# In 11 of 64 attention units, one maximum step that takes two key blocks

## The chip, the cores and the metric

The kernel runs on one core of a Trainium2 chip. A core has five engines with a queue of instructions each: TensorE (PE, matrix products into PSUM), VectorE (DVE), ScalarE (ACT), GpSimd (POOL, no access to PSUM here) and SyncE (SP, which issues DMA transfers). They run at the same time and wait for one another through semaphores. The metric is the time of one execution on the device in microseconds (us); lower is better.

## The reference

The kernel computes one transformer block on x of 2048 tokens by 512 channels, in bfloat16: layer norm, attention with 32 heads of 16 channels, a projection with a residual, layer norm, and a gated feed-forward part of 1792 channels with a residual. Cut to what matters:

```python
q, k, v = qkv[0], qkv[1], qkv[2]
scores = jnp.einsum("bhqd,bhkd->bhqk", q, k) * (Dh ** -0.5)
p = _softmax(scores, axis=-1)
o = jnp.einsum("bhqk,bhkd->bhqd", p, v)
...
h = x + _A_ref(_layernorm(x, axis=-1), A_wqkv, A_wo)
h2 = h + _B_ref(_layernorm(h, axis=-1), B_w_gate, B_w_up, B_w_down)
```

where `_B_ref` is `(gelu(x @ w_gate) * (x @ w_up)) @ w_down`. The softmax needs, for each query and head, the maximum of 2048 scores.

## The kernel before, in words

**Units.** Attention is cut into 64 units. A unit is 256 queries (one of 8 groups `gi`) by 4 heads (one of 8 `slot`s; the heads' 16 channels sit in row groups of 32 partitions). Each unit goes through two passes.

**Pass 1, the maxima.** For each of 16 steps j, two matmuls (`p1_pair`, L797) write the scores of 128 queries and 512 keys for two heads into two PSUM banks, and VectorE takes both maxima in one reduction of 128 x 1024 (`p1_consume`, L806). The step's number says which block it is: key block kc = j // 4 (of four), query tile qh = (j // 2) % 2, head pair j % 2. GpSimd joins the four key blocks' maxima (`negm_part`, `negm_pre`), writes the negative maximum as three bfloat16 parts, has it transposed by a DMA (`negm_post`, L846) and adds it to spare rows of the queries (L851), so that a later product of keys and queries gives the score less the maximum.

**Pass 2, the exponentials.** 24 ticks after a unit's first maximum step, its scores are computed again with keys as rows (`p2_tile`, L867), and ScalarE takes the exponential of 128 x 512 per tile (`p2_consume`, L879). The tiles go into a ring of 34 buffers; `item_pv` (L893) multiplies them with the values (a column of ones gives the sums). Every other unit, `item_ofin` turns the result with fp32 transposes on TensorE (L919), ScalarE copies it (OAT, L641), and GpSimd divides by the sums with a power of -1 (L928) and a product (L932).

**Ticks.** The main loop from L1293 writes out one tick per maximum step: first the scores of pass 1, then two tiles of pass 2, then one piece of a dense stream (`Dense.piece`): projections of queries, keys and values, the value products, the output projection, and the gate, up and down products of the feed-forward part of an earlier group. If no piece may start, `dummy` (L1285) puts in matmuls without a use. PSUM has eight banks: two pairs for pass 1 in turn, four for pass 2 and the dense pieces together. The order of each engine's instructions is fixed when the program is built. A planner decides it with estimated costs: `act_lag` counts how far ScalarE would be behind at 1.135 us a tick, and gate and up pieces start only under `LAG_START`; `PoolStream` has a budget for GpSimd; `defer` places an operation some ticks later; `ADDX` is the delay before L851.

**The end.** After the last maximum step, 24 ticks of exponentials are left, then `tail_a` and `tail_b`: the last normalisation, output projection, layer norm and feed-forward part of the last group, with `fill` putting pieces or dummies into TensorE's waits. `FILL_2` and `FILL_LN` say how many. `evac_act` (L641) copies out of PSUM on ScalarE, or on VectorE (L630) once the maxima are done.

Of the kernel before, what the change touches and what calls it, by code (L numbers as in the profile page):

```python
# [222 lines left out]
ADDX = 4  # L223
# [3 lines left out]
FILL_2 = 4  # L227
FILL_LN = 16
LAG_START = 0.4
LAG_OP = 0.2  # L230
TANH_LAG = 2


def bass_sequential_preLN__mha_block__geglu_ffn__prompt_kernel(nc, A_x, A_wqkv, A_wo, B_x, B_w_gate, B_w_up, B_w_down, out):
    dbg = None
    with ExitStack() as es:
# [74 lines left out]
        OAT = at("OAT", [128, 2, 272], FP32)  # L311
# [189 lines left out]
        def startable(it, room):  # L501
            if it[0] is item_gate and par_busy[it[1][1] % 2] and room < 10:
                return False
            if it[0] is item_down and it[1][0] == GL - 1 and not force[0]:
                return False
# [4 lines left out]
        class Dense:  # L510
            def __init__(self):
                self.prio = []
                self.ready = []
                self.gen = None
                self.bank = None
                self.banks = [7, 3, 4, 5]
                self.rr = 0
                self.pause = 0
                self.single = False
                self.done = 0  # L520
                self.now = 0
# [6 lines left out]
            def _start(self, item):  # L528
                genfn, a, est, nb = item
                if self.single:  # L530
# [5 lines left out]
            def piece(self):  # L536
                if self.single and self.pause > 0:
                    return 0
                while True:
                    if self.gen is None:  # L540
# [4 lines left out]
                        if self.prio and (not self.single or self.prio[0][3] <= self.now):  # L545
                            self._start(self.prio.pop(0))
                        elif self.ready and (not self.single or ((act_lag[0] <= LAG_START or force[0] or self.ready[0][0] not in (item_gate, item_up)) and startable(self.ready[0], lim - self.now) and self.ready[0][3] <= self.now and self.now + self.ready[0][2] + PAUSE - 1 <= lim)):
# [3 lines left out]
                    try:  # L551
# [11 lines left out]
                        if self.single:  # L563
                            banks.give(self.bank)
                            self.pause = PAUSE
# [7 lines left out]
        dense = Dense()  # L573

# [19 lines left out]
        class PoolStream:  # L594

            def __init__(self):
                self.q = []
                self.budget = 0.0
            def add(self, ops, then=None):
# [4 lines left out]
            def spend(self, cost):  # L604
                self.budget -= cost
            def run(self, flush=False):
                while self.q and (flush or self.budget >= min(self.q[0][0], 1.0)):
                    if not flush and self.q[0][0] > 2.0 and dense.now % 16 in (1, 2, 3, 13, 14, 15):
                        break
                    cost, fn, then = self.q.pop(0)  # L610
                    self.budget -= cost
                    fn()
# [190 lines left out]
        def p1_consume(ui, tiles):  # L803
            par = ui % 2
            (b, qt, kc, g), (b2, _, _, g2) = tiles
            P.op("dve", lambda e: e.tensor_reduce(out=PM[:, par, qt, kc, g:g + 2], in_=pbank[:, b:b + 2, :], axis=AX.X, op=ALU.max),  # L806
                 reads=[("pb", b), ("pb", b2)], writes=[("PM", par, qt, kc, g), ("PM", par, qt, kc, g2)])

        def negm_part(ui, k):
# [10 lines left out]
            else:  # L820
# [3 lines left out]
                P.op("pool", lambda e: e.tensor_scalar(out=m3, in0=m3, scalar1=-1.0, scalar2=None, op0=ALU.mult), reads=[("MXm", par)], writes=[("MXm", par)])  # L824

# [16 lines left out]
        def negm_post(ui):  # L842
# [10 lines left out]
            defer(ADDX, add)  # L853
# [6 lines left out]
        def p2_tile(ui, j, gp, jj):  # L860
# [3 lines left out]
            m, g, b = j // 2, 2 * gp + jj, banks.take()  # L864
# [5 lines left out]
            return (b, m, g)  # L870

# [10 lines left out]
        def item_pv(b, ui):  # L882
# [18 lines left out]
            evac_act(OA[:, par, 256 * col:256 * col + 256], pbank[:, b, 0:256], [("pb", b)], [("OA", par, col)], cost=0.41)  # L901
            if gi == GL and slot >= NSLOT - 2:
                if col == 0:
                    dense.add(item_ofin, gi, (slot,), front=True, est=3, not_before=dense.now + 3)
            elif col == 1:
                dense.add(item_ofin, gi, (slot - 1, slot), front=True, est=3, not_before=dense.now + 3)
# [6 lines left out]
        oat_busy = {}  # L913
        def item_ofin(b, gi, slots):
            gp, par, ns = gi % 2, slots[0] // 2 % 2, len(slots)
            assert not oat_busy.get(par), "GpSimd too far behind"
            for q in range(2):
                for sp in range(ns):
                    P.op("pe", lambda e, q=q, sp=sp: e.transpose(out=pbank[:, b, 128 * (q * ns + sp):128 * (q * ns + sp) + 128], in_=OA[:, par, 256 * sp + 128 * q:256 * sp + 128 * q + 128], identity=ident32[:]),  # L919
# [487 lines left out]
```

## Time and profile before

| what | us |
|---|---|
| median of 3 runs | 1243.94 (1243.86 to 1244.21) |
| the profiled execution, its own time | 1243.15 |
| its span, first to last instruction | 1241.4 |
| first maximum step starts | 14.66 |
| last maximum step ends | 1184.92 |
| last exponential ends | 1211.33 |
| VectorE, busy in maxima | 1162.4 |
| ScalarE, busy in exponentials | 1102.9 |

The span is 1.75 us shorter than the execution's time. The 1102.9 us are the sum of three groups of the page by the tile that they write (737.0 + 228.2 + 137.7 for PTM, PTG and PTE, one ring). A group's line gives line, engine, operation, tiles and shapes, then the busy time, the mean duration of one in ns, and the idle time before them with what ended it. An instruction's duration on ScalarE and VectorE overlaps the next one's, so a sum of durations is more than an engine needs; the chain of waits, in which each piece begins where the one before ends, has no such overlap.

### The profile page before, as it was taken

How to read it: one execution, taken by the hardware profiler on the slowest of the kernel's cores; microseconds unless marked ns; L12 is line 12 of the kernel's file. 1: busy time of each engine (PE TensorE's matmuls, PEld its weight loads, DVE VectorE, ACT ScalarE, POOL GpSimd, SP SyncE). 2: the span in 40 equal slices, each digit the busy share in tenths (PEclk: the TensorE clock that was granted, in tenths of full speed). 3: DMA queues.
4: the chain of work that ended last, by engine and by line, in shares of the span. 5: the costliest groups of instructions: out<-in, count | busy, mean ns of one | idle time of the engine just before them, and what ended most of it. 6: DMA issues, size and time to landing. Idle time of an engine off the chain costs nothing.

```text
span 1241.4 us, 31438 instructions
## 1 busy us (share of the span) xinstructions
PE 1137.8 (92%) x12680; PEld 437.8 (35%) x12680; DVE 1189.8 (96%) x1088; ACT 1199.9 (97%) x2464; POOL 764.3 (62%) x1540
## 2 busy tenths in 40 slices
PE   7999888899999999999999998999999999999998
PEld 3333222233333333333333333333333333333335
DVE  8999999999999999999999999999999999999923
ACT  7899999999999999999999999999999999999992
POOL 8647774467746765376645777367654766547760
PEclk9999999999999999999999999999999999999989
DMA  5101004300010000100010000100002000100000
GB/s 151 31 22 28 24 19 130 89 6 3 6 31 12 6 6 6 38 5 6 4 27 18 4 6 6 27 17 6 6 4 40 6 4 6 27 19 3 6 13 18
DMA packets 50800, 27.45 MB, mean 22 GB/s; under 512 B 36064, under 2 KB 49632, under 8 KB 50656
## 3 DMA queue, kind: packets, MB, share of 16 engines
q1 hardware_dynamic: 50656, 25.45, 8.0%
q8 instruction: 101, 1.65, 0.5%
q14 instruction: 43, 0.35, 0.1%
HBM read 11.80 MB, written 2.10 MB: 11 GB/s over the span
## 4 chain that ended last, share of the span: by engine, by line
DVE 58%; ACT 30%; PE 9%; POOL 2%; issue 1%; DMA 0%
DVE PM L806 57%; ACT PTM L879 17%; ACT PTG L879 5%; ACT PTE L879 3%; PE pbank L1122 2%; PE pbank L867 2%; PE pbank L797 1%; ACT th_sb L1055 1%; PE pbank L1072 1%; ACT g_sb L641 1%; ACT OnT L1012 1%; ACT u_sb L641 1%; PE pbank L739 1%; PE pbank L998 1%; PE pbank L676 1%
## 5 line engine op out<-in xcount | busy, mean ns | idle before, releaser
L806 DVE TENSOR_REDUCE PM<-pbank 128x2 f32<-128x1024 f32 x1024 | 1162.4, 1224 | 5.3 <-PE pbank L867 2.8
L879 ACT ACTIVATE PTM<-pbank 128x512 bf16<-128x512 f32 x1388 | 737.0, 669 | 4.7
L867 PE MATMUL pbank<-QT,KT 32*128 32x256 bf16 x4096 | 498.2, 273 | 9.7 <-ACT PTM L879 4.4
L797 PE MATMUL pbank<-KT,QT 32*128 32x512 bf16 x2048 | 394.2, 382 | 46.4 <-DVE PM L806 23.6
L1285 PE MATMUL pbank<-ones_bf,ident 128*128 128x512 bf16 x794 | 245.3, 384 | 28.1 <-ACT PTM L879 3.2
L797 PEld LDWEIGHTS pbank<-KT,QT 32*128 32x128 bf16 x2048 | 104.5, 91 | 392.7 <-DVE PM L806 170.3
L879 ACT ACTIVATE PTG<-pbank 128x512 bf16<-128x512 f32 x420 | 228.2, 660 | 1.1 <-PE pbank L867 0.3
L867 PEld LDWEIGHTS pbank<-QT,KT 32*128 32x128 bf16 x4096 | 164.5, 92 | 65.7 <-ACT PTM L879 36.8
L879 ACT ACTIVATE PTE<-pbank 128x512 bf16<-128x512 f32 x240 | 137.7, 667 | 1.9 <-PE pbank L867 1.1
L893 PE MATMUL pbank<-PTM,VA 128*17 128x256 bf16 x2776 | 125.8, 274 | 2.7 <-ACT PTM L879 1.2
L832 POOL TENSOR_TENSOR MX<-PM,MX 128x8 f32<-128x8 f32 x64 | 12.9, 202 | 163.9 <-DVE PM L806 163.9
L1285 PEld LDWEIGHTS pbank<-ones_bf,ident 128*128 128x128 bf16 x794 | 47.6, 97 | 131.4 <-ACT PTM L879 83.8
L928 POOL TENSOR_TENSOR LINV<-OAT,negone 128x16 f32<-128x16 f32 (+1 forms) x32 | 92.7, 2896 | 0.0
L893 PEld LDWEIGHTS pbank<-PTM,VA 128*17 128x17 bf16 x2776 | 60.1, 89 | 46.9 <-issue 29.1
L821 POOL TENSOR_TENSOR MX<-PM,MX 128x8 f32<-128x8 f32 x64 | 13.0, 203 | 101.5 <-DVE PM L806 101.5
L1072 PE MATMUL pbank<-hnT_l,wu_sb 128*128 128x256 bf16 x448 | 67.1, 276 | 3.1 <-ACT PTM L879 0.2
L1072 PE MATMUL pbank<-hnT_l,wg_sb 128*128 128x256 bf16 x448 | 66.9, 275 | 2.5
L1114 POOL TENSOR_TENSOR GUT<-th_sb,u_sb 128x512 bf16<-128x512 f32 x49 | 62.2, 1270 | 5.1 <-DVE u_sb L630 3.0
L1061 POOL TENSOR_TENSOR th_sb<-th_sb,g_sb 128x512 f32<-128x512 f32 x49 | 62.1, 1268 | 4.1
L1064 POOL TENSOR_TENSOR th_sb<-th_sb,g_sb 128x512 f32<-128x512 f32 x49 | 62.1, 1268 | 3.1
L1062 POOL TENSOR_TENSOR th_sb<-g_sb 128x512 f32<-128x512 f32 x49 | 51.0, 1041 | 18.8 <-ACT g_sb L641 18.8
L1122 PE MATMUL pbank<-wd_sb,GUT 128*128 128x512 bf16 x224 | 60.5, 382 | 0.6 <-ACT PTM L879 0.2
(149 smaller groups left out, 1077.3 us busy)
## 6 DMA issues: line engine op xcount, KB each, us to landing
QKS<-QKS SPq DMA_DIRECT2D x27, 112.0 KB, 2.2
x_sb<-in_A_x_dram SPq DMA_DIRECT2D x4, 512.0 KB, 5.6
xres<-in_A_x_dram SPq DMA_DIRECT2D x16, 128.0 KB, 2.2
out_dram<-out_sb SPq DMA_DIRECT2D x16, 128.0 KB, 1.8
wg_sb<-in_B_w_gate_dram SPq DMA_DIRECT2D x4, 448.0 KB, 5.0
wu_sb<-in_B_w_up_dram SPq DMA_DIRECT2D x4, 448.0 KB, 4.0
wd_sb<-in_B_w_down_dram SPq DMA_DIRECT2D x3, 512.0 KB, 6.4
STG<-ST SPq DMA_TRANSPOSE x64, 2.3
```

What stands on the lines that cost most here:

```text
L797: P.op("pe", lambda e, g=g, b=b: e.matmul(pbank[:, b, :], QT[32 * g:32 * g + 32, c, slot, 128 * qt:128 * qt + 128], KT[32 * g:32 * g + 32, ...
L806: P.op("dve", lambda e: e.tensor_reduce(out=PM[:, par, qt, kc, g:g + 2], in_=pbank[:, b:b + 2, :], axis=AX.X, op=ALU.max), reads=[("pb", b ...
L867: P.op("pe", lambda e, kt=kt, i=i: e.matmul(pbank[:, b, 256 * i:256 * i + 256], KT[32 * g:32 * g + 32, slot, 128 * kt:128 * kt + 128], QT[ ...
L879: P.op("act", lambda e, b=b, pi=pi: e.activation(out=PTt(pi), in_=pbank[:, b, :], func=ACT.Exp), reads=[("pb", b)], writes=[("PT", pi)], e ...
L893: P.op("pe", lambda e, g=g, kt=kt, pi=pi, i=i: e.matmul(pbank[32 * g:32 * g + 17, b, 0:256], VA[:, kt, 4 * slot + g, :], PTt(pi)[:, 256 * ...
L928: P.op("pool", lambda e: e.tensor_tensor(out=li, in0=oat4[:, :, :, 16], in1=negone[:, 0:8 * ns].rearrange("p (q h) -> p q h", q=2), op=ALU ...
L1061: o(1.27, lambda e: e.tensor_tensor(out=ts_, in0=ts_, in1=gs, op=ALU.mult), [("th", par), ("g", par)])], then=done)
L1064: o(1.27, lambda e: e.tensor_tensor(out=ts_, in0=ts_, in1=gs, op=ALU.mult), [("th", par), ("g", par)])], then=lambda: defer(TANH_LAG, lamb ...
L1072: P.op("pe", lambda e, dc=dc, fc=fc, i=i: e.matmul(pbank[:, b, 256 * i:256 * i + 256], w[:, dc, 128 * fc:128 * fc + 128], hT[:, dc, :], st ...
L1114: P.op("pool", lambda e: e.tensor_tensor(out=o_ap, in0=shp(ts_), in1=shp(us), op=ALU.mult), reads=[("th", par), ("u", par)], writes=o_keys ...
L1122: P.op("pe", lambda e: e.matmul(pbank[:, b, :], GUT[:, fc, 128 * k:128 * k + 128], wd_sb[:, fc, :], start=first, stop=last), reads=[("GUT" ...
L1285: P.op("pe", lambda e: e.matmul(pbank[:, b, :], ident[:], ones_bf[:, 0:512], start=True, stop=True), reads=["ident", "ones_bf"], writes=[( ...
```

## The change

11 units (`JOINT`: 12, 15, 18, 22, 26, 30, 34, 38, 42, 46, 50) have 15 maximum steps where they had 16. For the second query tile and the first head pair, key blocks 2 and 3 are taken together:

- In time before, GpSimd writes the negative of 128 queries (`joint_prep`, QN). For each of the two heads, two matmuls add up in one bank: scores of block 3 less scores of block 2 (`item_diff`). ScalarE writes the positive part to SBUF (Relu, RB).
- At step 10, which held block 2 alone, VectorE runs for each head a fused instruction: scores of block 2 from PSUM plus RB, and the maximum over the 512 columns. That is the maximum over both blocks, since a + max(b - a, 0) = max(a, b).
- Step 14, which held block 3, is left out, and with it its tick. The pass 2 tiles of that tick (two) are made up by three tiles in odd ticks after it (`behind`). GpSimd copies the maximum to block 3's place.

With it go other edits. Each unit's result is written as bfloat16 (OB) and turned by a DMA (`o_turn`); GpSimd normalises it per unit (`o_norm`), so the fp32 transposes and the OAT copies of the pairs of units go, and one `item_ofin` is left at the end. Maxima are joined at steps 9 and 13 instead of 8 and 12, and `unit_end` puts a unit's end at the head of the next tick. `tight` holds dense pieces back around the left-out tick; limits of the planner are set anew. In the end, exponentials go in pairs of tiles where their buffers adjoin (`p2_pair`, 128 x 1024), the first down product of group 6 may run in the loop, the first part of the last projection (`tail_a2`) stands after the last value product, the last normalised tile is copied by two engines in halves, and the numbers of filling matmuls change.

```diff
-ADDX = 4
+ADDX = 3
...
-FILL_2 = 4
-FILL_LN = 16
-LAG_START = 0.4
+FILL_2 = 5
+FILL_LN = 13
+LAG_START = 0.3
...
+JOINT = (12, 15, 18, 22, 26, 30, 34, 38, 42, 46, 50)
+J_AT, J_GONE = 10, 14
+LAG_EXTRA = 0.2
...
-            if it[0] is item_down and it[1][0] == GL - 1 and not force[0]:
+            if it[0] is item_down and it[1] == (GL - 1, 1) and not force[0]:
+                return False
+            if it[0] is item_down and not force[0] and (tight() or dense.now // 16 in JOINT and dense.now % 16 > J_GONE - 6 or act_lag[0] > LAG_START):
                 return False
...
+        def tight():
+            return dense.now // 16 in JOINT and dense.now % 16 >= J_GONE - 2 or bool(behind[0])
...
+            if ui in JOINT and (qt, kc, g) == (1, 2, 0):
+                assert y_left[ui] == 0, "differences too late"
+                for b_, g_ in ((b, g), (b2, g2)):
+                    P.op("dve", lambda e, b_=b_, g_=g_: e.tensor_tensor_reduce(out=RB[:, g_, :], in0=pbank[:, b_, :], in1=RB[:, g_, :], scale=1.0, scalar=-3.0e38, op0=ALU.add, op1=ALU.max, accum_out=PM[:, par, qt, kc, g_:g_ + 1]),
+                         reads=[("pb", b_), ("RB", g_)], writes=[("PM", par, qt, kc, g_), ("RB", g_)])
+                return
...
+        def p2_pair(ui, tiles):
...
+            if q1 == q0 + 1 and pt_tiles[q0][0] is pt_tiles[q1][0]:
+                o_ap = pt_tiles[q0][0][:, pt_tiles[q0][1]:pt_tiles[q0][1] + 2, :]
+                P.op("act", lambda e: e.activation(out=o_ap, in_=pbank[:, b0:b0 + 2, :], func=ACT.Exp), reads=[("pb", b0), ("pb", b1)], writes=[("PT", q0), ("PT", q1)])
...
-            elif col == 1:
-                dense.add(item_ofin, gi, (slot - 1, slot), front=True, est=3, not_before=dense.now + 3)
+            else:
+                evac_act(OB[:, ui % 2, :], pbank[:, b, 0:256], [("pb", b)], [("OB", ui % 2)], cost=0.27, then=lambda: o_turn(ui))
...
+        def o_turn(ui):
...
+            P.dma("sp", lambda e: e.dma_start_transpose(out=OBT[:, par, :, :], in_=OB[:, par, :]), ("obT", par), reads=[("OB", par)], writes=[("OBT", par)])
+            o4 = OBT[:, par].rearrange("p q (g i) -> p q g i", i=32)
+            defer(5, lambda: o_norm(gi, slot, par, o4, ("OBT", par), ob_busy))
...
+            pool.add([(1.45, inv), (0.31, mul)], then=over)
...
+        def joint_prep(ui):
...
+            pool.add([(0.4, lambda: P.op("pool", lambda e: e.tensor_scalar(out=QN[:], in0=QT[:, c, slot, 128 * qt:128 * qt + 128], scalar1=-1.0, scalar2=None, op0=ALU.mult),
+                                         reads=[("qT", slot, c, gi % 2)], writes=["QN"]))], then=lambda: defer(1, lambda: dense.extra.extend([(item_diff, (ui, g), 2, 0) for g in (0, 1)])))
+
+        def item_diff(b, ui, g):
...
+            P.op("pe", lambda e: e.matmul(pbank[:, b, :], QT[32 * g:32 * g + 32, c, slot, 128 * qt:128 * qt + 128], KT[32 * g:32 * g + 32, slot, 1536:2048], start=True, stop=False, tile_position=(32 * g, 0)),
+                 reads=[("qT", slot, c, hf), ("kT", slot, 3)], writes=[("pb", b)], sig=False)
+            P.op("pe", lambda e: e.matmul(pbank[:, b, :], QN[32 * g:32 * g + 32, :], KT[32 * g:32 * g + 32, slot, 1024:1536], start=False, stop=True, tile_position=(32 * g, 0)),
+                 reads=["QN", ("kT", slot, 2)], writes=[("pb", b)], sig=True)
+            act_more(0.48)
+            P.op("act", lambda e: e.activation(out=RB[:, g, :], in_=pbank[:, b, :], func=ACT.Relu), reads=[("pb", b)], writes=[("RB", g)], extra_deps=dG)
...
+            if p1_ok and tick // 16 in JOINT and tick % 16 == J_GONE:
+                for i, (k_, fn_) in enumerate(deferred):
+                    deferred[i] = (k_ + 1, fn_)
+                behind[0] += 2
+                tick += 1
+                dense.now = tick
+                continue
...
+            more = 1 if behind[0] and tick % 2 else 0
...
-                if tick % 16 in (8, 12):
+                if tick % 16 in (9, 13):
...
             fill(FILL_LN)
-            for k in (0, 1):
-                in_bank(tail_hnT, k)
-            fill(2)
+            sp_ = [b for b in range(2, 8) if b not in (own, other)]
+            tail_hnT(sp_[0], 0, (0, 1, 2, 3), "dve")
+            tail_hnT(sp_[1], 1, (0, 1), "act")
+            tail_hnT(sp_[2], 1, (2, 3), "dve")
```

## The prediction

> **What bounds the kernel now.** I read the page's busy shares first, then the costliest groups, then the chain of waits, and last the busy time by stretch, cut where the maximum steps show a stage to begin.
>
> ```profile
> PE 1137.8 (92%) x12680; PEld 437.8 (35%) x12680; DVE 1189.8 (96%) x1088; ACT 1199.9 (97%) x2464; POOL 764.3 (62%) x1540
> ...
> L806 DVE TENSOR_REDUCE PM<-pbank 128x2 f32<-128x1024 f32 x1024 | 1162.4, 1224 | 5.3 <-PE pbank L867 2.8
> ```
>
> VectorE is one long row of 1024 maxima. But ScalarE has the same busy share, so the shares alone cannot say which of the two sets the pace. The chain over the whole run can:
>
> ```profile
> 413.15 91.72 DVE PM L806 x81
> 515.89 2.94 ACT PTM L879 x6
> 527.03 2.97 ACT PTG L879 x6
> 532.94 4.50 ACT PTM L879 x9
> ...
> 558.88 91.72 DVE PM L806 x81
> ```
>
> Its pattern comes back every 145.73 us (413.15 to 558.88), which is eight units, 128 maximum steps. For 91.7 us of it the chain stays on VectorE, at 91.72 / 81 = 1.132 us a step (I use 1.131, the distance of two starts in the timeline), for the other 54 us it runs through ScalarE and TensorE. A close look at one such place gives what each ScalarE instruction really takes when one follows another:
>
> ```profile
> 522.55 0.28 ACT OA L641
> 522.82 1.47 ACT PTM L879 x3
> 524.29 1.96 ACT PTE L879 x4
> 526.25 0.49 ACT PTG L879
> 526.74 0.29 ACT OAT L641
> 527.03 2.97 ACT PTG L879 x6
> ```
>
> An exponential takes 1.96 / 4 = 0.490 us (the groups' mean of 669 ns overlaps the next one), the copy out of a value product 0.28, the copy after its transposes 0.29. By stretches of eight units, and then the end:
>
> ```profile
> 383.61:529.34 145.73, 134.59 (x1550) 51.54 (x1548) 145.19 (x129) 144.76 (x300) 90.22 (x186) 1.00 0.06 13
> 529.34:675.09 145.75, 134.63 (x1550) 51.58 (x1548) 145.21 (x130) 144.77 (x300) 90.22 (x186) 1.00 0.05 12
> 1184.92:1211.33 26.41, 23.94 (x261) 9.89 (x261) 3.36 (x6) 24.79 (x50) 19.61 (x24) 0.87 0.05 14
> 1211.33:1241.42 30.09, 27.04 (x193) 17.70 (x193) 10.89 (x22) 8.06 (x13) 0.70 (x1) 1.00 0.05 18
> ```
>
> Columns: length, then busy time of TensorE, weight loads, VectorE, ScalarE, GpSimd, then TensorE's clock. Eight units need 128 x 1.131 = 144.8 us of VectorE. Of ScalarE they need 256 exponentials x 0.490 = 125.4, 18 copies of 512 x 0.490 = 8.8, 7 tanh x 0.52 (starts in the timeline) = 3.6, two squares and two copies with their sums 1.4, 8 x 0.28 = 2.2 and 4 x 0.29 = 1.2, together 142.6. So VectorE bounds the loop by 2.1 us in eight units, 1.0 us is lost to stalls, and ScalarE has 1.5% to spare, no more. After the last maximum come 26.4 us of remaining exponentials, then 30.1 us of last projection, second norm and feed-forward.
>
> **The change part by part.**
>
> *VectorE, in 11 units.* Two steps go, 2 x 1.131 = 2.26 us; two fused add-and-maximum instructions of 512 columns come, each with an instruction that reads the accumulator. No row shows that operation. Nearest is the product at L1101 (one PSUM and one SBUF operand, 512 columns): 0.692 us alone. A maximum step shows 1.224 and moves on after 1.131, so 0.09 of a duration overlaps: 0.60. For the accumulator read, ScalarE's reads add 0.09 and VectorE's smallest aggregate shows 0.17: 0.09 to 0.17. I take 0.73 for the two; bounds 0.60 (read free) and 0.87 (nothing overlaps). A far bound, if two fp32 sources ran at half the rate of a maximum: 512 x 2 x (1.131 / 1024) + 0.09 = 1.22. So 0.73 x 2 = 1.46 replaces 2.26: 0.80 less, 8.8 us in 11 units.
>
> *ScalarE.* Each of those units adds two Relu of 512 columns, at a copy's 0.49: 22 x 0.49 = 10.8 us. All units but the last two lose the fp32 transposes, and with them 31 copies x 0.29 = 9.0 us; one is left. The built order of ScalarE has its two table loads where they were, so Relu brings none.
>
> *The two together.* I counted both engines' instructions unit by unit in the built order, with the durations above. Units 12 to 63, before: VectorE 941.0, ScalarE 928.1, measured 237.56 to 1184.92 = 947.4. After: VectorE 932.2, ScalarE 932.4. They are level; whatever ScalarE is short of in one unit, VectorE waits. If ScalarE's lag could be made up anywhere within eight units, the larger of the two sums per eight units counts: 941.0 before, 935.1 after, 5.9 less. If it had to be made up within its unit, the larger sum of each unit counts: the excesses of ScalarE add to 3.8 us before (units 13, 15, and 20, 21 of each eight) and 11.7 after (largest: 0.85 in units 25, 33, 41, 49 and 1.2 in unit 51, where transferred feed-forward work now falls): 944.8 against 943.8, 1.0 less. The chain shows lags of some exponentials passing from unit to unit, but not over many, so I take the middle: **3.5 us less in the loop**, ends 1.0 and 5.9.
>
> *The tick that is left out.* Its two exponentials are made up after it, 3 + 2 + 3 in three ticks: 8 x 0.49 = 3.92 us against 3 x 1.131 = 3.39. The 0.53 is about one of the four banks for exponentials, and feed-forward pieces are held back there; that ring hides it. With a lag already standing it would show: at most 11 x 0.53 = 5.8 us, which would bring the forecast to 1243.0.
>
> *TensorE.* 44 matmuls of the differences come; 22 of the dropped steps and 122 small fp32 transposes of 0.30 us go. It is 92% busy with 792 dummy matmuls still among its work. In its queue the next step's scores stand behind a difference, which waits for a bank as any feed-forward piece does. Cost nothing; with the cover gone it is part of the lag counted above.
>
> *GpSimd and the SyncE queue.* Normalisation per unit: 62 x (1.65 + 0.40) against 31 x (2.90 + 0.62), 18 us more on an engine with 477 us idle, and its two waits for maxima (L821 and L832, 101 and 164 us) move one step later. 62 more DMA transposes, at 1.17 us of queue each, stand ahead of the query transposes in the SyncE queue. A query's chain needs 7 x 0.22 + 2.3 + 0.67 = 4.5 us from its unit's end and is used 8 ticks, 9.0 us, later: one collision of 1.2 is covered, three would show. Cost nothing.
>
> *The end.* 22 pairs of exponentials in one instruction: the copies of 1024 and 512 columns show 1022 and 597 ns, so a pair takes 0.49 + 0.425 = 0.915, 0.065 less than two. With one tanh fewer: 22 x 0.915 + 4 x 0.49 + 0.52 = 22.6 against 48 x 0.49 + 2 x 0.52 = 24.6: 1.9 less. Of the 1.9 us that ScalarE idles there, part belongs to the low clock:
>
> ```profile
> 1194.00:1198.00 4.00, 3.11 (x24) 1.20 (x20) 0.86 (x2) 3.81 (x9) 3.75 (x6) 1.00 0.00 0
> 1198.00:1199.30 1.30, 0.80 (x6) 0.23 (x6) 0.00 (x0) 1.30 (x4) 1.30 (x2) 1.00 0.02 6
> 1199.30:1206.10 6.80, 6.76 (x37) 2.00 (x34) 0.00 (x0) 5.40 (x12) 5.01 (x5) 0.50 0.00 0
> ```
>
> TensorE runs at half clock for 6.8 us after thinner work, and ScalarE idles 1.4 us in it. The new order has three dummies where it had two. I take half: 0.7 less, bounds 0 and 1.4. The Trainium skill ("TensorE: Matmul & The Clock Gate", Part 1) says that the clock halves after an idle window of some 3.4 us; the 6.8 us agree with two such windows, the 3.11 busy of 4.00 ahead of them with no idle one. By it the 1.4 would go whole or stay whole. After the last exponential: transposes at 1218.44 stand behind filler while their input is there at 1217.88, and one copy of 0.60 is split over two engines: 0.6 less. **End: 3.2 us less**, bounds 2.0 and 4.0.
>
> Sum: the profiled execution took 1243.15 (span 1241.4 and 1.75 around it), 1243.15 - 3.5 - 3.2 = 1236.45; the median of the runs stands 0.79 above that execution: **1237.2 us**.
>
> **The rivals.**
> - *ScalarE eats the loop's gain*: every lag must be paid in its unit. For it: sums level, eight stretches alike with 1.0 lost even now. Against: the chain passes lags on. 1243.94 - 1.0 - 3.2 = 1239.7.
> - *VectorE's saving comes whole*: for it, ScalarE's stretches in the chain show no idle; against, it has nothing left to spare. 1243.94 - 8.8 - 3.2 = 1231.9.
> - *The fused step is slow, and the kernel with it*: at 1.22 us each the 11 units lose 0.18 apiece on VectorE (+2.0), the same lags stay: between +2.0 and +8.9 by the two ways of counting, middle +5.4, less 3.2: 1246.1. It decides from about 1.1 us a piece. For it: no such row at all, fp32, two sources and an accumulator. Against: L1101 reads the same pair of memories in 0.692. The Trainium skill ("Vector Engine (DVE) Microarchitecture Reference", Points that are easy to get wrong) halves the throughput of this family when both sources are non-bf16 in SBUF; here one is in PSUM, so by its words it would not strike, and no run here shows it.
>
> **How the numbers follow.** Forecast 0.55, lags paid in their unit 0.20, whole saving 0.08, slow fused step 0.12, else 0.05. 0.2% (2.5 us) is about what can be told from no change. Faster holds the first three, 0.83; the slow step is split by its price, same 0.09, slower 0.08. The range reaches from near the whole saving, 1233.0, past the eaten gain with the end's worse bound, 1242.0.
>
> **What would show it.** Groups: 1002 maxima, 22 fused rows near 0.7 us, Relu as a copy; VectorE's step at the fused pair 1.4 to 1.5 us. Stretches of eight units with two joint steps: 144.5 to 145.2 in place of 145.75, VectorE's waits for TensorE grown. Last maximum near 1181.4, last exponential near 1205, then 29.5 to the end, no half clock. Wrong if the fused rows pass 1.1 us, if eight units stay at 145.7, or if units after 50 lose more than 2 us.

## The result, and the profile after

The changed kernel takes **1246.10 us** (median of 17 runs, 1243.13 to 1248.24); the kernel before, on the same chip, 1243.98 (17 runs, 1243.25 to 1244.74). The ratio is 1.0017, 95% interval 1.0010 to 1.0024: slower by 2.1 us, within the 0.2% that I had set for "no change", where I forecast 1237.2 and a range up to 1242.0. The runs also spread over 5.1 us where they spread over 1.5.

The profiled execution took 1245.19 us (span 1243.4). The page's busy times, the maxima's group, and the groups of the line of the fused step (RB lies in the tile OA, and the trace names it so):

```profile
PE 1139.0 (92%) x12576; PEld 428.5 (34%) x12576; DVE 1181.6 (95%) x1107; ACT 1198.4 (96%) x2437; POOL 787.0 (63%) x1624
...
L836 DVE TENSOR_REDUCE PM<-pbank 128x2 f32<-128x1024 f32 x1002 | 1144.1, 1217 | 17.0 <-PE pbank L899 12.8
```

```profile
L833 DVE CUSTOM_DVE_ANT_0 OA<-pbank,OA 128x512 f32<-128x512 f32 x22 | 14.2, 683 | 0.0
L833 DVE DVE_READ_ACCUMULATOR2_ANT PM<- 128x1 f32 x22 | 1.8, 83 | 0.0
```

The change does what it says: 22 maxima fewer, 22 fused steps. VectorE's timeline at one joint step (start, duration) shows their real price:

```profile
429.55 1.22 DVE L836 TENSOR_REDUCE PM<-pbank 128x2 f32<-128x1024 f32 x1
430.68 0.68 DVE L833 CUSTOM_DVE_ANT_0 OA<-pbank,OA 128x512 f32<-128x512 f32 x1
431.28 0.08 DVE L833 DVE_READ_ACCUMULATOR2_ANT PM<- 128x1 f32 x1
431.28 0.69 DVE L833 CUSTOM_DVE_ANT_0 OA<-pbank,OA 128x512 f32<-128x512 f32 x1
431.89 0.08 DVE L833 DVE_READ_ACCUMULATOR2_ANT PM<- 128x1 f32 x1
431.89 2.35 DVE L836 TENSOR_REDUCE PM<-pbank 128x2 f32<-128x1024 f32 x2
```

From start to start a fused step takes 0.60 to 0.61 us, its accumulator read within it. So VectorE has 22 x (1.131 - 0.606) = 11.55 us less to do. Yet the last maximum ends at 1190.97 instead of 1184.92. The idle time that the page puts before the maxima has gone from 5.3 to 17.0 us, and the page's chain is mostly ScalarE's now:

```profile
ACT 57%; DVE 22%; PE 12%; POOL 5%; issue 3%; DMA 2%; POOLq 0%; DVEq 0%
```

Before it was DVE 58% and ACT 30%. Busy time by stretch (columns as before), eight units with two joint steps each in the first two lines, then eight units in which something more happens, then the two parts of the end:

```profile
529.41:675.20 145.79, 135.72 (x1533) 50.78 (x1533) 144.05 (x132) 144.81 (x299) 93.54 (x198) 1.00 0.07 16
675.20:821.01 145.81, 135.71 (x1533) 50.77 (x1533) 144.04 (x132) 144.81 (x299) 93.55 (x198) 1.00 0.07 16
821.01:969.26 148.25, 136.83 (x1533) 50.68 (x1532) 144.33 (x132) 145.39 (x301) 95.65 (x206) 0.99 0.07 16
...
1190.97:1214.25 23.28, 21.92 (x268) 8.90 (x268) 1.98 (x5) 23.02 (x28) 10.59 (x16) 1.00 0.07 21
1214.25:1243.40 29.15, 26.03 (x188) 17.11 (x188) 9.80 (x21) 8.44 (x14) 0.70 (x1) 1.00 0.05 15
```

Eight units take 145.8 us as before, with VectorE's own need in them down by 2.1. In a ledger of the two profiled spans ("stalls" is the time from a unit's first maximum step to the next unit's, less that unit's steps at 1.131 and 0.606):

| part | before | after | difference |
|---|---|---|---|
| start of the first maximum | 14.66 | 14.97 | +0.3 |
| VectorE's own steps | | | -11.55 |
| stalls, units 0 to 11 | 5.75 | 6.14 | +0.4 |
| stalls, units 12 to 63 | 6.28 | 23.19 | **+16.9** |
| last maximum to last exponential | 26.41 | 23.28 | -3.1 |
| last exponential to the end | 30.09 | 29.15 | -0.9 |
| sum (spans: +2.0) | | | +2.0 |

The question is where 16.9 us of stalls come from.

### The profile page after: what moved, and what is told of

It reads as the page before. It is cut to its first block, busy times and chain, and to the rows that moved or that the text cites. A ratio compares the mean times of both kernels' runs of the same rounds, so it can differ in the third digit from the quotient of the medians.

```text
span 1243.4 us, 31405 instructions
## 1 busy us (share of the span) xinstructions
PE 1139.0 (92%) x12576; PEld 428.5 (34%) x12576; DVE 1181.6 (95%) x1107; ACT 1198.4 (96%) x2437; POOL 787.0 (63%) x1624
## 4 chain that ended last, share of the span: by engine, by line
ACT 57%; DVE 22%; PE 12%; POOL 5%; issue 3%; DMA 2%; POOLq 0%; DVEq 0%
ACT PTM L928 32%; DVE PM L836 22%; ACT PTG L928 10%; ACT PTE L928 5%; PE pbank L1207 3%; PE pbank L1367 2%; PE pbank L821 2%; PE pbank L899 2%; ACT th_sb L1137 2%; ACT g_sb L665 2%; ACT u_sb L665 1%; DMA STG<-ST 1%; PE pbank L1157 1%; ACT OB L665 1%; POOL LINV L976 1%
## 5 line engine op out<-in xcount | busy, mean ns | idle before, releaser
L836 DVE TENSOR_REDUCE PM<-pbank 128x2 f32<-128x1024 f32 x1002 | 1144.1, 1217 | 17.0 <-PE pbank L899 12.8
L899 PE MATMUL pbank<-QT,KT 32*128 32x256 bf16 x4096 | 518.2, 273 | 17.0 <-ACT PTM L928 6.6
L821 PE MATMUL pbank<-KT,QT 32*128 32x512 bf16 x2026 | 389.6, 384 | 24.9 <-DVE PM L836 11.9
L1367 PE MATMUL pbank<-ones_bf,ident 128*128 128x512 bf16 x792 | 239.0, 384 | 31.6 <-ACT PTM L928 3.3
L821 PEld LDWEIGHTS pbank<-KT,QT 32*128 32x128 bf16 x2026 | 97.8, 91 | 365.0 <-DVE PM L836 125.5
L899 PEld LDWEIGHTS pbank<-QT,KT 32*128 32x128 bf16 x4096 | 172.4, 92 | 90.6 <-ACT PTM L928 47.5
L883 POOL TENSOR_TENSOR QT<-QT,STG 128x256 bf16<-128x256 bf16 x64 | 42.8, 669 | 129.4 <-DMA STG<-ST 129.4
L976 POOL TENSOR_TENSOR LINV<-OBT,negone 128x8 f32<-128x8 bf16 x62 | 103.5, 1669 | 0.1
L736 POOL TENSOR_SCALAR QT<-QKS,qmask 128x512 bf16<-128x512 bf16 x30 | 46.9, 1568 | 11.4 <-ACT QKS L665 9.7
```

The costliest lines, as they stand in the source:

```text
L821: P.op("pe", lambda e, g=g, b=b: e.matmul(pbank[:, b, :], QT[32 * g:32 * g + 32, c, slot, 128 * qt:128 * qt + 128], KT[32 * g:32 * g + 32, ...
L899: P.op("pe", lambda e, kt=kt, i=i: e.matmul(pbank[:, b, 256 * i:256 * i + 256], KT[32 * g:32 * g + 32, slot, 128 * kt:128 * kt + 128], QT[ ...
L976: P.op("pool", lambda e: e.tensor_tensor(out=li, in0=o4[:, :, :, 16], in1=negone[:, 0:8].rearrange("p (q h) -> p q h", q=2), op=ALU.pow), ...
L1367: P.op("pe", lambda e: e.matmul(pbank[:, b, :], ident[:], ones_bf[:, 0:512], start=True, stop=True), reads=["ident", "ones_bf"], writes=[( ...
```

## The experiments

Three theories stood against each other. **A**: the DMA transposes (62 more, and each consumer placed a fixed number of ticks behind its issue) make GpSimd and TensorE wait. **B**: ScalarE has nothing to spare, so the Relus come back as stalls. **C**: the planner's new limits put the feed-forward work into too few units. The runs were made in four groups, on four chips, so times of different groups are compared by their distance from the kernel before in the same group: 1243.43 (`e1` to `e4`), 1243.95 (`e5` to `e8`), 1243.42 (`e9` to `e12`) and 1243.71 (`e13` to `e15`). After the change that distance is +2.1.

**The added ScalarE work alone.** To the kernel before, 22 Relus that nobody waits for:

```diff
+            if p1_ok and tick // 16 in (12, 15, 18, 22, 26, 30, 34, 38, 42, 46, 50) and tick % 16 in (4, 9):
+                P.op("act", lambda e: e.activation(out=RIN[:], in_=RIN[:], func=ACT.Relu), reads=["RIN"], writes=["RIN"])
```

> The kernel before with nothing changed but 22 instructions more on ScalarE: a Relu of 512 columns on a tile of its own, two in each of the 11 units that have a joint step after the change, behind the exponentials of the unit's steps 4 and 9. No engine waits for them, and the order of everything else is as before. This asks by itself what my term for the two engines together took the middle of: can ScalarE make up 10.8 us over eight units, of which it has some 2 to spare, or is each lag paid by VectorE in its unit. Made up: the sums of eight units say at most 0.3 us for each group with two such units, 1 to 2 us in all, 1245 to 1246. Paid at once (theory B in its hard form): 22 x 0.49 less what its own unit has free, 6 to 10 us, 1250 to 1254.

1250.55 (1250.26 to 1250.97), ratio 1.0057 [1.0040, 1.0073]: **+7.1 us**. Its chain of waits in one of those units, and its eight units:

```profile
427.84 0.51 ACT RIN L1346
428.35 1.47 ACT PTM L881 x3
429.82 1.99 ACT PTE L881 x4
431.81 0.49 ACT PTG L881
432.30 0.52 ACT th_sb L1057
432.81 0.97 ACT PTG L881 x2
433.79 0.52 ACT RIN L1346
```

```profile
532.92:679.95 147.03, 136.52 (x1550) 52.16 (x1548) 145.95 (x130) 146.23 (x304) 89.95 (x186) 1.00 0.05 12
```

A Relu takes 0.51 to 0.52 here, so 22 of them are 11.3 us, and 63% of that is paid. Four in eight units are 2.06 us, and the eight units grow by 1.28. My sum had ScalarE's need in eight units at 142.6 and VectorE's at 144.8; by that the four had room, and they were paid for nonetheless. No other engine has more to do here, so this run shows by itself that added ScalarE work costs time in this loop although its total would fit.

**The differences left out.** The changed kernel without the 44 matmuls and the 22 Relus:

```diff
-            P.op("pe", lambda e: e.matmul(pbank[:, b, :], QT[32 * g:32 * g + 32, c, slot, 128 * qt:128 * qt + 128], KT[32 * g:32 * g + 32, slot, 1536:2048], start=True, stop=False, tile_position=(32 * g, 0)),
...
-            P.op("pe", lambda e: e.matmul(pbank[:, b, :], QN[32 * g:32 * g + 32, :], KT[32 * g:32 * g + 32, slot, 1024:1536], start=False, stop=True, tile_position=(32 * g, 0)),
...
-            P.op("act", lambda e: e.activation(out=RB[:, g, :], in_=pbank[:, b, :], func=ACT.Relu), reads=[("pb", b)], writes=[("RB", g)], extra_deps=dG)
```

> The changed kernel without the 44 difference matmuls and the 22 Relu (the fused step adds a buffer that starts at zero, so block 3 of that query tile is left out of the maximum); everything else in its place. Theory A: ScalarE's 10.8 us were not what lengthened the loop; 1 to 4 us less than the changed kernel, and the stalls around units 26, 34, 42 and 50 stay. Theory B: 9 us or more less, 1237 or below, and those stalls go.

1240.69 (1238.43 to 1241.49), ratio 0.9974 [0.9963, 0.9985], a distance of -2.7: 4.9 us better than with them, between the ranges of the two theories. Their ScalarE time is 22 x 0.49 = 10.8, and 4.9 is some 45% of it; the 44 matmuls went with them, so the 4.9 are the price of the differences as a whole. The stalls in units 12 to 63 are still 17.1 us of the 23.19 (in the fastest of the seven executions, 2.3 us under their median): the differences come back as stalls, as B says, and are not all.

**No joint step.**

```diff
-JOINT = (12, 15, 18, 22, 26, 30, 34, 38, 42, 46, 50)
+JOINT = ()
```

> The changed kernel with no joint unit: all other edits stay (transposes by DMA, the query addition 3 ticks after a unit, the new planner limits, the end). Theory A (the DMA transposes set the pace: GpSimd stands at the query addition L883 for each transposed maximum, TensorE stands at the output projection for its transposed input): the stalls come with these other edits, so the loop stays as long as with joint steps or gets longer, with 1024 maxima x 1.131 = 1158 plus 20 us or more of stalls, and the wait at L883 stays near 130 us; total 1245 to 1252. Theory B (ScalarE has nothing to spare, so the joint steps' Relu and the 3 + 2 + 3 exponentials cost what VectorE saves): without them VectorE bounds the loop as before, 1170, and the better end gives 1240.

1249.63 (1249.54 to 1250.06), ratio 1.0049 [1.0032, 1.0066]: **+6.2**. So the edits that came with the joint steps make the kernel slower, and the joint steps win back 4.1 of it, or a third of VectorE's 11.55. In the loop alone it is more: the last maximum ends at 1196.16, 11.2 us later than before, and the better end hides a part. Two runs split the 6.2. The one with the addition of the query back at 4 steps and the new limits kept:

```diff
-ADDX = 3
+ADDX = 4
...
+JOINT = ()
```

> No joint step, the new limits for feed-forward work kept, the query addition at 4 steps as before the change. Between the run with no joint step alone (1249.6: new limits, addition at 3) and the one with before's limits and the addition at 4 (1243.2) lie 6.4 us; this run splits them. If the limits carry it (theory C): 1248 to 1250, with feed-forward work bunched in units 20 to 23 of each eight as there. If the addition's step carries it (theory A: three steps are too few for a query chain that waits for the transposes): 1243 to 1245.

1248.48 (1247.81 to 1249.46), ratio 1.0038 [1.0023, 1.0053]: +4.8. The other with the addition at 4 and before's limits as well, so that of the loop's edits the results turned by DMA are left, with the places of the joined maxima and GpSimd's budget:

```diff
-LAG_START = 0.3
+LAG_START = 0.4
...
-            if it[0] is item_down and not force[0] and (tight() or dense.now // 16 in JOINT and dense.now % 16 > J_GONE - 6 or act_lag[0] > LAG_START):
+            if it[0] is item_down and not force[0] and (tight() or dense.now // 16 in JOINT and dense.now % 16 > J_GONE - 6):
...
-                if not force[0] and (act_lag[0] + (0.48 if dense.gen is not None and dense.cur in (item_gate, item_up) else 0) > LAG_TH + SLOPE * n or poly_end[par] > 1.135 * dense.now + POLY):
+                if not force[0] and act_lag[0] > LAG_OP + 0.1 * n:
```

> No joint steps, the query addition at 4 steps and the limits for feed-forward work (start 0.4, old rule for the gate's product, no rule for the down projection) as before the change. What is left of the loop's edits is the results turned by DMA instead of TensorE (and the places of the negated maxima, one step later). Theory A (the transposes in the SyncE queue, with GpSimd standing at the query transposes): the wait of GpSimd for them stays over 70 us, eight units stay over 146.3, time 1243 to 1250. Theory C (the new limits bunch the feed-forward work on ScalarE): the stalls go back to about 1 us in eight units, time 1239 to 1241. Theory B (ScalarE level) expects C's number too, since ScalarE has 9 us less to do than before.

1243.22 (1242.34 to 1244.54), ratio 0.9994 [0.9984, 1.0003]: -0.7. By the time that is theory A's range, by its best eight units (145.70) it is C's. So the new limits, without joint steps, cost 4.8 + 0.7 = 5.5 us, and the earlier addition 1.4. The -0.7 itself is made of two: 52.2 us follow the last maximum instead of 56.5, but it ends at 1188.39, 3.5 us later than before, although ScalarE has 31 copies less to make. Eight units of the first run of this group (no joint step, all else as changed) and of the last:

```profile
386.70:533.65 146.95, 128.18 (x1518) 49.23 (x1540) 145.68 (x130) 144.81 (x297) 92.29 (x195) 1.00 0.07 16
```

```profile
384.50:530.20 145.70, 129.18 (x1519) 49.61 (x1540) 145.10 (x129) 144.40 (x296) 91.73 (x195) 1.00 0.07 16
```

The same instructions on ScalarE (296 or 297), 1.25 us apart. In the first, 1.85 of 2.17 us of stalls lie in units 20 to 23, the first half of the eight; that is what C says. That the limits do the same harm beside joint steps is not shown: before's limits with joint steps were not run.

**The end.** The loop as before, and only the new end:

```diff
-FILL_2 = 4
-FILL_LN = 16
+FILL_2 = 5
+FILL_LN = 13
...
-            defer(ADDX, add)
+            defer(ADDX + (ui == NU - 1), add)
...
+        def p2_pair(ui, tiles):
```

> The loop of the kernel before, with only the new end: pairs of exponentials in one instruction, no pause between feed-forward pieces after the last maximum, three projections early, the split copies, fillers of 5 and 13. No joint steps, the fp32 transposes on TensorE as before, before's limits. Last maximum as before (1184.9 to 1185.4), and what follows it 52.4 us as after the change instead of 56.5, if the end's gain is its own: 1239.4 us. If the shorter end needs the new loop (feed-forward work that is left over differs), 1241 to 1243. This is also the base against which the loop's edits are to be judged: if it is 1239.4, the changed loop costs 6.7.

1244.52 (1243.37 to 1245.51), ratio 1.0004 [0.9995, 1.0014]: **nothing gained**, and 57.1 us after the last maximum instead of 56.5. ScalarE's timeline shows two gelus (tanh) left to do after it, and a wait before the first:

```profile
1194.82 0.63 ACT L1072 ACTIVATE th_sb<-th_sb 128x512 f32<-128x512 f32 x1 [1.67 <-POOL th_sb L1081]
1198.97 0.65 ACT L1072 ACTIVATE th_sb<-th_sb 128x512 f32<-128x512 f32 x1
```

In the changed kernel there is one (at 1195.13). The same holds for every run here with the results turned by DMA: with one left, 52.1 to 52.6 us follow the last maximum (ten kernels, the changed one among them), with two left 55.4 (four kernels, told below). Without the wait of 1.67 this run would be there too: 57.1 - 1.67 = 55.4. So of the end's 4.1 us some 3.0 go together with one piece pair of the feed-forward part that the loop no longer leaves over. The wait of 1.67 comes from GpSimd, whose timeline has the last query's addition behind a normalisation of two units and a feed-forward piece:

```profile
1187.49 2.93 POOL L945 TENSOR_TENSOR LINV<-OAT,negone 128x16 f32<-128x16 f32 x1
1190.50 0.62 POOL L949 TENSOR_TENSOR Otok<-OAT,LINV 128x256 bf16<-128x256 f32 x1
1191.08 1.04 POOL L1079 TENSOR_TENSOR th_sb<-g_sb 128x512 f32<-128x512 f32 x1
1192.08 0.67 POOL L851 TENSOR_TENSOR QT<-QT,STG 128x256 bf16<-128x256 bf16 x1
```

**The transposes.** In the changed kernel GpSimd waits for the query transposes in all 64 units (129.4 us, against 19.4 in 19 waits before), and the chain of waits goes through two late ones where two units lose the most:

```profile
933.39 3.66 DMA STG<-ST
937.04 0.07 issue
937.11 0.67 POOL QT L883
937.78 1.63 POOL LINV L976
...
944.09 3.69 DMA OnT<-Otok
947.79 0.05 issue
947.83 0.61 PE pbank L1076 x2
```

Everything of the output projection hangs on the first one, since GpSimd normalises behind the query's addition. TensorE then stands 1.7 us for the second, and the granted clock falls (busy time by stretch, the clock third from the right):

```profile
948.90:952.30 3.40, 3.40 (x17) 0.72 (x16) 2.35 (x2) 2.65 (x6) 2.44 (x8) 0.51 0.00 0
```

Units 50 and 51 lose 4.0 us together (1.9 when both consumers are moved, below). Three runs move the consumers. The query's addition alone, two steps later:

```diff
-ADDX = 3
+ADDX = 5
```

> The changed kernel with the query addition 5 ticks after a unit (3) alone. Theory A: the larger part of what both edits give, 3 to 7 us less than the changed kernel, the wait at L883 below 20 us; what stays is TensorE at the output projection. Theory B: within 1.5 us of the changed kernel.

1246.35 (1244.95 to 1247.25), ratio 1.0023 [1.0012, 1.0033], +2.9: GpSimd's wait falls to 80.2 us and the time does not. An engine that would be idle anyway may wait at no cost. The output projection alone:

```diff
-            dense.add(item_oproj, gi, k, front=True, est=3, not_before=dense.now + 4)
+            dense.add(item_oproj, gi, k, front=True, est=3, not_before=dense.now + 6)
```

> The changed kernel with the output projection 2 steps later (6 instead of 4) and the query addition where it is (3). With both moved the time fell by 3.6 us, with the addition alone moved it stayed. If the whole 3.6 is TensorE standing at the output projection for its DMA-turned input: 1242.5, and the wait of GpSimd for the query transposes stays near 130 us, costing nothing. If both are needed: 1244 to 1246.

1246.09 (1243.60 to 1247.49), ratio 1.0019 [1.0010, 1.0029], +2.7, nothing gained either. TensorE's weight loads there wait 0.9 us instead of 5.8, and the stalls in units 12 to 63 are 1.5 us fewer, but the end has two tanh left. One unit lost 3.3 us in this execution; its chain begins with a query transpose that landed late:

```profile
693.88 4.13 DMA STG<-ST
698.08 0.67 POOL QT L883
698.74 1.01 POOL th_sb L1147
```

Both together:

> The changed kernel with the query addition 5 ticks after a unit (3) and the output projection's earliest start 6 ticks after its transposes are issued (4). No work added or taken away. Theory A: the wait at L883 falls from 129 us to below 20, the chain no longer runs through the transposes, 6 to 10 us less than the changed kernel: 1236 to 1240. Theory B: the same work on ScalarE, so within 1.5 us of the changed kernel, 1245 to 1247.

1242.47 (1241.77 to 1242.97), ratio 0.9991 [0.9982, 1.0000], -1.0: 3.1 us better than the changed kernel by the distances, although two tanh are left here too, and a spread of 1.2 us instead of 5.1. That lies between the two ranges. The last maximum comes at 1185.39, 5.6 us earlier than in the changed kernel; with the addition alone it came at 1191.82, with the projection alone at 1189.20, so it takes both. A holds for the places where TensorE waits and where a late transpose has no margin, as far as the chains above tell, and not for GpSimd's idle time.

**How many joint steps.** With the two places moved and the threshold of the gate's product from 0.2 to 0.1:

```diff
-LAG_TH = 0.2
+LAG_TH = 0.1
```

> The changed kernel with 11 joint steps; the query addition 2 steps later (5), the output projection 2 later (6), and the threshold of the gate's product at 0.1 in place of 0.2, so that its pieces are put where ScalarE's lag is smaller. Theory A: as with the first two alone, 1242.5. Theory C: the third takes 2 to 4 us of stalls out of the units where feed-forward work falls beside a joint step (34, 42, 50, 51): 1238 to 1240.5. Theory B (no room at all in 11 units): 1242.5, stalls of 3 us in eight units wherever they fall.

1242.99 (1241.75 to 1244.56), ratio 0.9992 [0.9983, 1.0001], -1.0: no better than with the two. The same with six joint steps:

```diff
-JOINT = (12, 15, 18, 22, 26, 30, 34, 38, 42, 46, 50)
+JOINT = (16, 24, 32, 40, 48, 56)
```

> As the run with the three places, but 6 joint steps instead of 11, at units 16, 24, 32, 40, 48 and 56, one in each eight. VectorE saves 6.3 us instead of 11.55; ScalarE gets 12 Relu of 0.49 instead of 22, 4.9 us less. Theory B: with one joint step in eight units ScalarE's total is below VectorE's again, stalls of 1 to 1.5 us in eight units, time 1234 to 1237, faster than with 11. Theory A alone: the saving lost and nothing gained, 1243 to 1247.

1238.86 (1238.64 to 1240.74), ratio 0.9962 [0.9949, 0.9975]: **-5.1 us, and faster with fewer**. And with none:

> The three places (addition 5, output projection 6, threshold 0.1) with no joint step: the third point of a row with 6 (1238.9) and 11 (1243.0). Without joint steps VectorE has 6.3 us more to do than with six. If ScalarE had room for one joint step in eight units and none for two, this is the old balance: 1243 to 1245, and six are the best of the three. If stalls in the six-joint run came from the joint steps too: 1240 to 1242.

1245.69 (1244.61 to 1246.19), ratio 1.0017 [1.0008, 1.0027]. This control isn't clean: TensorE stands 9.2 us in six places there for the transposed second norm, which the run with six does in one place, for 2.9 us (its waits; us in total, times, longest):

```profile
PEld pbank L1157 <- DMA hnT_l<-OnT: 2.9, 1, 2.9
```

That one wait is taken out by beginning the feed-forward part later:

```diff
-                defer(3, lambda: add_ffn_when(gi))
+                defer(5, lambda: add_ffn_when(gi))
```

> The run with six joint steps lost 2.96 us in unit 59, where TensorE stood 2.9 us at the first gate weights for the DMA-turned second norm, as it stood for the turned results at the output projection. Here the feed-forward of a query tile is begun two steps later (5 instead of 3 after that transpose is issued), nothing else. If the stall is only that wait: 1236.0, unit 59 under 0.5 us, no wait of TensorE for that transpose. If it moves elsewhere: 1238 to 1239.

**1236.01 us** (1235.84 to 1236.55), ratio 0.9941 [0.9926, 0.9956], the fastest of this study; unit 59 loses 0.37 instead of 2.96. From here, 11 joint steps evenly placed:

```diff
-JOINT = (16, 24, 32, 40, 48, 56)
+JOINT = (16, 20, 24, 28, 32, 36, 40, 44, 48, 52, 56)
```

> As the run of 1236.0 us, but with 11 joint steps again, evenly every four units from 16 to 56. Apart from the number of joint steps nothing differs, so the difference is what five more of them bring: VectorE 5.25 us less, ScalarE 10 Relu of 0.49, 4.9 us more. ScalarE with nothing to spare (theory B): the saving is eaten by lags, 1236 to 1240. If the eleven lost only by their places beside feed-forward work: 1231 to 1234.

1243.72 (1242.78 to 1243.82), ratio 0.9998 [0.9988, 1.0007]: 7.4 us lost again, more than theory B foresaw. And five at other places:

```diff
+JOINT = (22, 30, 38, 46, 54)
```

> As the run of 1236.0 us, with five joint steps at units 22, 30, 38, 46 and 54 (one in each eight, six units later in it, beside other feed-forward work, none in the first group). If only the number in eight units counts: 1236.5 to 1238 (1.05 less saved). If the place beside the feed-forward work counts as much: outside of that, either way.

1237.24 (1237.12 to 1237.39), ratio 0.9947 [0.9932, 0.9962]. That is 0.9 us behind the six by the distances, with one joint step, 1.05 us of VectorE, fewer: between these two choices of place hardly anything changes, and the number counts. Fewer than five, or seven to ten, were not run. Eight units with one joint step (the run of 1236.0), then with two (11 even ones):

```profile
528.76:673.77 145.01, 134.27 (x1538) 50.32 (x1537) 144.50 (x131) 144.24 (x298) 92.41 (x196) 1.00 0.07 16
```

```profile
529.37:675.40 146.03, 130.62 (x1509) 50.66 (x1532) 144.21 (x133) 145.15 (x300) 92.99 (x198) 1.00 0.07 16
```

The second joint step takes 1.05 us off VectorE, puts 0.95 on ScalarE (two Relus of 0.477 from start to start), and the eight units grow by 1.02. In the loop that makes 4.4 us (last maximum at 1186.29 against 1181.86); another 3.3 are the end, where two tanh are left instead of one.

## Why the prediction was wrong

Three of the runs lie one after the other between before and after. Their last maxima (before: 1184.92) show what each step did to the loop:

| what is added | last maximum | to the one above |
|---|---|---|
| results turned by DMA, joined maxima a step later, the new end | 1188.39 | +3.5 |
| the planner's new limits | 1194.02 | +5.6 |
| the query's addition after 3 ticks instead of 4 | 1196.16 | +2.1 |
| 11 joint steps: the changed kernel | 1190.97 | -5.2 |

So the joint steps bring 5.2 us of VectorE's 11.55, and the edits around them cost 11.2, where my sum had them cost nothing in the loop. In another order the steps could share this out otherwise. Taken from the changed kernel instead, of the 16.9 us of stalls the differences answer for 6.1 (17.1 are left without them) and the places behind the transposes for 6.0 (17.1 with both moved); the two need not add. The rest, some 5, is of the size of what the limits cost, but they were not tried with joint steps.

**A price in my sums was wrong.** I took 0.490 us for an exponential from the chain, whose pieces run from end to end. Ends drift, because the durations shown grow by about 0.01 us from one instruction to the next; and the four that I divided held a wait. So the chain is not free of the overlap. From start to start, at the same place in the kernel before (start, duration of the group):

```profile
522.70 1.59 ACT L879 ACTIVATE PTM<-pbank 128x512 bf16<-128x512 f32 x3
524.13 2.12 ACT L879 ACTIVATE PTE<-pbank 128x512 bf16<-128x512 f32 x4
526.13 0.62 ACT L879 ACTIVATE PTG<-pbank 128x512 bf16<-128x512 f32 x1
```

Three exponentials take 1.43 us, 0.477 each; the next four take 2.00, mostly because the fourth stood for its scores. In the eight units from 529.34 on, 220 of 256 exponentials are followed within 0.50 us, at 0.477 or 0.478 in most cases. The other 36 are followed 6.0 us later in sum than that, and at 35 of them TensorE had just ended a score product of pass 2 (L867). So ScalarE needs 139.0 us there, not 142.6. With a copy of 512 and a Relu of the differences at 0.477, OAT at 0.277 and the added Relu at 0.52, eight units need and take:

| kernel | VectorE | ScalarE, my sums | ScalarE, by starts | took | over VectorE |
|---|---|---|---|---|---|
| before | 144.77 | 142.6 | 139.0 | 145.75 | 1.0 |
| before's limits, DMA-turned, no joint step | 144.77 | 141.4 | 137.9 | 145.70 (others to 146.84) | 0.9 (2.1) |
| one joint step (1236.0) | 143.72 | 142.4 | 138.8 | 145.01 | 1.3 |
| before and four Relus | 144.77 | 144.7 | 141.1 | 147.03 | 2.3 |
| two joint steps (11 even ones) | 142.67 | 143.4 | 139.8 | 146.03 | 3.4 |

- **"The two together", "3.5 us less in the loop, ends 1.0 and 5.9", is the step that failed.** Measured: 6.0 more (1184.92 to 1190.97). Both ends compared sums of work of the two engines, took the larger and left the loss over it as it was. The sums were not level: by starts ScalarE needs 909 us in units 12 to 63 after the change and VectorE 929. ScalarE had 4% to spare, not 1.5%, and it was not to be had all the same. The loss over VectorE's sum rises from 1.0 to 3.4 us in eight units while ScalarE's sum is still 3 to 7 us below. The last two rows are each one edit away from the first and the third, and lose 1.3 and 2.1 us more than these. The order counts beside the sums: with the second row's work and the new limits eight units take 146.95, 2.2 over VectorE. In all five ScalarE stands 5 to 7 us in eight units for TensorE's scores, and VectorE waits for TensorE too (14.4 of its 17.0 us in the changed kernel), which in turn waits for banks that ScalarE has not emptied (47.5 us at the weights of pass 2's scores, L899, for exponentials of PTM). That the pauses of the one and the lags of the other fall in different ticks is how I read this; no run moved them apart.
- **"GpSimd and the SyncE queue ... Cost nothing" failed second.** I counted the queue's 1.17 us and the chain's 4.5 against 9.0. But the output projection, 4 steps behind its transpose, had no cover, and the landing is no constant: transposes that landed 1.1 to 1.3 us late stopped TensorE and took the clock with it. Price: 3.1 us, by the run with both places moved. The lateness is not new: in the kernel before, 6 of 64 query transposes landed 3.25 to 4.02 us after their issue. What is new is that the query's addition stands 3 ticks behind them instead of 4, and each unit's normalisation behind that.
- **The planner's new limits were no term of the sum.** Without joint steps they cost 5.5 us, more than all that I had the loop gain. I had counted instructions unit by unit in the built order, and had seen lags of 0.85 and 1.2 in five units; what the new order did in the other units I had not asked.
- *VectorE, in 11 units*: 0.73 a step, measured 0.606, at my lower bound (read free). 11.55 us saved instead of 8.8: the error was on the other side.
- *ScalarE*: the counts were right, and a Relu takes the same as an exponential, 0.477 from start to start. The 31 copies that went brought nothing by themselves: the loop without them and without joint steps is 3.5 us longer.
- *The tick that is left out*, "that ring hides it": open. With the differences left out the stalls stay at 17.1 us, and this burst is one of the things still in them, but no run separates it.
- *The end*: 3.2 forecast, 4.1 measured (56.5 to 52.4), by another cause than mine. The edits of the end alone gave nothing; 3.0 are the piece pair that is no longer left over. Of the half clock, TensorE shows 1.00 from the last maximum to the last exponential, so my 0.7 went as I had bounded it, at its better end. The rule of the Trainium skill ("TensorE: Matmul & The Clock Gate", Part 1), by which it would go whole or stay whole, agrees with that, and its window of some 3.4 us with the 3.40 us at 948.9. Its condition, a whole idle window, does not agree: TensorE stood 1.7 us ahead of these 3.40, and no longer.
- *The rivals*: "ScalarE eats the loop's gain" named the mechanism and stopped at paying its own lags once (1239.7). "The fused step is slow" gave 1246.1, the measured time, and is wrong: 0.606, not 1.1. That it met the time is chance.

What would show it wrong was named rightly: "if eight units stay at 145.7" is what happened, and "if units after 50 lose more than 2 us" too (6.8, against 1.9 before).

## What to carry to other kernels

Where two engines take turns in every step, room in the sum of an engine's work does not make added work free: here 45% and 63% of the Relus' time were paid in two runs, with ScalarE's sum below VectorE's throughout. The best split here left ScalarE 4.9 us below VectorE in 145. Take an instruction's price from start to start, not from the ends in a chain of waits. Before pricing a transfer as hidden, ask for each consumer how many us stand between its issue and its use, and use the landing's worst cases, not its median. An edit to a planner's limits is a term of the sum as large as an instruction's: price it by building the version with the limits alone. The same holds for every edit that comes along with the main one.

## What the runs showed of the hardware that I had not expected

- The fused add-and-maximum of 512 fp32 columns, one source in PSUM and one in SBUF, moves on after 0.606 us, and its accumulator read (83 ns) adds nothing to that. A maximum of 1024 columns takes 1.131, so a column costs the fused step some 7% more than the plain one.
- A DMA transpose for the query's maximum lands 2.4 us after its issue in most cases (from the issue to GpSimd's next step, where GpSimd waited), and after 3.2 to 4.2 in 3 to 6 of 64, counted in four executions; the one of 4.13 above had no other transfer of its queue within 2.5 us ahead of it. The changed kernel's spread of 5.1 us, and 1.2 with both places moved, fits that; the spread itself was not traced run by run.
- An exponential of 128 x 512 from PSUM moves on after 0.477 us while its shown duration lies between 0.59 and 0.74 (515 to 533 us in the kernel before); the Relu of 128 x 512 bf16 from SBUF to SBUF takes 0.519.
- TensorE's clock was halved without a whole idle stretch. Ahead of the last 10 us it happened 15 times, in 12 of the 17 profiled executions, for 3.41 or 6.83 us; in the 3.41 us ahead of each TensorE was busy for 0.85 to 2.26 us by its rows, and its longest pause was 0.84 to 2.56 us.
